# p doubled earlier, the first W_in tiles in pairs by column half, idle products placed anew, and a new order of the words, in an attention and MLP kernel

## The chip, the cores and the metric

The kernel runs on one core of one Trainium2 chip. TensorE does the products, VectorE, ScalarE and GpSimd (POOL) the rest, and SyncE (SP) starts the output and transposing DMAs. The metric is device time in microseconds (us). The kernel before takes 259.2 us, the median of 7 runs (258.06 to 260.01).

## What is computed

```
def sm_attn(qq, kk, vv):               # softmax attention, scale 1/sqrt(64)
    ...
p_packed = sm_attn(p, k, v)            # 32 packed rows of each head
out = sm_attn(q, p_packed, p_packed)   # (8, 8, 576, 64)
x = out.transpose(0, 2, 1, 3).reshape(4608, 512)
h = x @ w_in                           # 512 x 2048
r = np.maximum(h, 0.0)
g = s * (r * r) + b
y = g @ w_out                          # 2048 x 512
```

8 batches, 8 heads, 576 rows, 64 columns in a head. All is given and returned in float32; the kernel computes in bf16 with float32 sums.

## The kernel before

Batches are done one after another, interleaved on TensorE by an order written out by hand: a list of words (lines 583 to 610), each run by `run` (line 509), which issues that step's instructions on every engine. Within an engine the order of the words is the order of execution; nothing is rearranged. The words, with the functions they call:

- `Lk`, `Lq`, `Lv`, `Lwi`, `Lwo`, `Lpall`, `Lsb`: loads, all started by POOL (lines 109 to 141). `Lwi` and `Lwo` load a quarter of W_in or W_out. k, q and v of batch 0, and p of batch 0, are started ahead of the list.
- `Tk`, `Tq`: transposes of half of k or q on TensorE (`on_pe`, line 185) through a PSUM tile, copied by VectorE to kT or qT. `Dk`, `Dq` do it by a transposing DMA from SP (`on_dma`, line 205), from batch 2 on.
- `PP`: p of batch 0 is doubled by VectorE (`twice`, line 146), transposed on TensorE and copied by ScalarE to pbd (line 149). `PPA` does the same for the p of batches 1 to 7 (pall, line 164); there VectorE and ScalarE each make two copies of the PSUM tile.
- `V`: v reordered to vr by VectorE (line 212).
- `F`: first scores for 4 heads, and their exp to e1 on ScalarE (line 220).
- `P`: packed products and their sums (line 244); behind the second half VectorE and ScalarE make rd, ppd and rs.
- `S`: second scores, and their exp to e2 (line 279). For batch 0 they are laid out by column half (of the 576 rows of q), so that the first half can go on alone.
- `A`: sums over each head's 32, then Ln and Exp on ScalarE and a product on VectorE, giving aT (lines 315 and 332).
- `W`: W_in times the packed values, scaled to pw (`packed_w`, line 344). For batch 0 one quarter at a time through two single-bank PSUM tiles (tag "y"), for the others two quarters through two double-bank tiles (tag "h").
- `M`: one tile of 128 of the 2048 columns: four products of pw and aT into a PSUM tile, Relu to rlu, square to gT (line 398). ScalarE does Relu, except for batch 0 where m % 4 = 2: there VectorE does.
- `h` (batch 0 alone): the same tile by column half, `h0.m.half` (line 381). Words `h0.0.0 h0.1.0`, then `h0.0.1 h0.1.1`; each is two products, a Relu and a square of 288 columns. M0.2 and M0.3 follow whole.
- `B`: products of W_out with ones for the bias; behind the last VectorE scales it by b to biasrep (line 422).
- `Ob.tx n`: n of the 16 products of one output tile; behind the sixteenth VectorE scales, adds biasrep and SP stores (line 445).
- `Z n`: n idle products of 128x512 zeros into a PSUM tile of their own (`idle`, line 498).

Two PSUM pools set what may run ahead. Tag "h" has two double-bank tiles (`big`, line 77): every T, PP, PPA, F, S, A, M and h takes one, so a step waits until the step two tiles earlier has been read out. Tag "y" has four single-bank tiles for O, B, P, Z and batch 0's W. gT and W_out are kept whole in SBUF; pw, aT and two kT and qT are double.

Of the kernel before, what the change touches and what calls it, by code (L numbers as in the profile page):

```python
# [14 lines left out]
def kernel(  # L15
# [18 lines left out]
    P = 128  # L34
# [26 lines left out]
    def mm(*a, **kw):  # L61
        return tc.keep_in_program_order(nc.tensor.matmul(*a, **kw))  # L62
# [11 lines left out]

    vec, act, pool, sp = (Pinned(e) for e in (nc.vector, nc.scalar, nc.gpsimd, nc.sync))

    def big(dt=F32):
        return psh.tile([P, 2, NB if dt == F32 else 2 * NB], dt, tag="h", name="hps")


# [65 lines left out]
    def twice(t):  # L146
        vec.tensor_copy(out=t[:, :, 1, :], in_=t[:, :, 0, :])

    def prep_p0():
        twice(pn)  # L150
        pt = big(BF16)
        for x in range(2):
            tr(
                pt[:, 0, x * P:(x + 1) * P],
                pn[:, x, :, :],
                identb[:],
            )
        for c2 in range(2):
            act.copy(
                out=pbd[D * c2:D * c2 + D, :, 0, :, c2, :],  # L160
                in_=pt[D * c2:D * c2 + D, 0, 0:2 * P].rearrange("p (g a j) -> p a g j", g=4, a=2),
            )
# [113 lines left out]
        rs[b] = smp.tile([P, 2], F32, tag="rs", name="rs")  # L276
        vec.tensor_scalar_mul(out=rs[b][:], in0=rd[b][:], scalar1=scale)

    def second_scores(b, by_half=False):
        e2[b] = attp.tile([P, 2, S], BF16, tag="e2", name="e2")  # L280
        tiles = [big() for _ in range(2)]
        for a in range(2):
            for g in range(4):
                for c2 in range(2):
                    t, i = (c2, a) if by_half else (a, c2)
                    mm(
                        tiles[t][NP * g:NP * g + NP, i, 0:HS],
                        ppd[b % 2][D * c2:D * c2 + D, a, g, :],
                        qT[b % 2][D * c2:D * c2 + D, head(a, g), :, :],
                        start=True,  # L290
                        stop=True,
                        tile_position=(D * c2, NP * g),
                    )
        if by_half:
            exp_half(b, tiles, 0, 0)
            exp_half(b, tiles, 1, 0)
            s2[b] = tiles
            return
        for a in range(2):
            act.activation(  # L300
                out=e2[b][:, a, :].rearrange("p (i s) -> p i s", i=2),
                in_=tiles[a][:, :, 0:HS],
                func=AF.Exp,
                scale=rs[b][:, a:a + 1],
            )
# [38 lines left out]
    def packed_w(b, chs):  # L344
        if chs[0] == 0:
            pw[b] = atp.tile([P, 2, DFF], BF16, tag="pw", name="pw")
        if len(chs) == 2:
            at = {(a, x): (a, x) for a in range(2) for x in range(2)}
            tiles = [big() for _ in range(2)]
        else:  # L350
            at = {(a, 0): (a, 0) for a in range(2)}
            tiles = [psy.tile([P, 1, NB], F32, tag="y", name="wps") for _ in range(2)]
        for x, ch in enumerate(chs):
            for g in range(4):
                for a in range(2):
                    t, i = at[a, x]
                    mm(
                        tiles[t][NP * g:NP * g + NP, i, :],
                        ppd[b % 2][D * a:D * a + D, a, g, :],
                        w_in_sb[D * a:D * a + D, g, ch * NB:(ch + 1) * NB],  # L360
                        start=True,
                        stop=True,
                        tile_position=(D * a, NP * g),
                    )
        for a in range(2):
            t, i0 = at[a, 0]
            src = tiles[t][:, i0:i0 + len(chs), :]
            dst = pw[b][:, a, chs[0] * NB:(chs[-1] + 1) * NB].rearrange("p (i f) -> p i f", f=NB)
            if a == 0 and (b, chs[0]) != (0, 0):
                act.activation(out=dst, in_=src, func=AF.Copy, scale=rd[b][:, a:a + 1])  # L370
            else:
                vec.tensor_scalar_mul(out=dst, in0=src, scalar1=rd[b][:, a:a + 1])


    def slot(b):
# [3 lines left out]
        return 0 if (b % 4) in (1, 2) else NT * P  # L379

    def mlp_in_half(b, m, hf):
        if hf == 0:
            pps[b, m] = big()
        hps = pps[b, m]
        for a in range(2):
            mm(
                hps[:, hf, 0:HS],
                pw[b][:, a, m * P:(m + 1) * P],
                aT[b][:, a, hf * HS:(hf + 1) * HS],
                start=(a == 0),  # L390
                stop=(a == 1),
            )
        rlu = ysp.tile([P, HS], BF16, tag="rluh", name="rluh")
        act.activation(out=rlu[:], in_=hps[:, hf, 0:HS], func=AF.Relu)
        g0 = slot(b) * S + hf * HS
        vec.tensor_tensor(out=gT[:, m, g0:g0 + HS], in0=rlu[:], in1=rlu[:], op=ALU.mult)

    def mlp_in(b, m):
        hps = big()
# [98 lines left out]
    def idle(n, cols=P):  # L498
# [3 lines left out]
        for _ in range(n):  # L502
            mm(zps["t"][:, 0:cols], zb[:, 0:P], zb[:, 0:cols], start=True, stop=True)


    todo = {(b, t): o for b in range(B) for t, o in enumerate(outs(b))}
    todo[B - 1, NT].cuts = (0, NB // 2, NB)

    def run(word):
        what = word.rstrip("0123456789.x-")  # L510
        n = [int(x) for x in word[len(what):].replace("x", ".").replace("-", ".").split(".") if x]
        if what == "Z":
            idle(n[0], NB)
        elif what in ("Lk", "Lq", "Lv"):
            h0, h1 = (4 * n[1], 4 * n[1] + 4) if len(n) == 2 else (0, H)
            load(what[1], n[0], h0, h1)
# [7 lines left out]
            load_w_out(4 * n[0], 4 * n[0] + 4)  # L524
        elif what == "Lsb":
            load_sb()
        elif what == "PP":
            prep_p0()
        elif what == "PPA":
# [51 lines left out]
    idle(12, NB)  # L581

    for word in """
        Lwi0 Lwi1 Lwi2 Lwi3 Lwo0 Lwo1 Lpall Tk0.0 Z10 Tk0.1 Lk1 Lwo2 PP0 V0.0 Z7 F0.0 F0.1 V0.1 Z5 P0.0
        P0.1 Tq0.0 Tq0.1 Lq1 Lwo3 Lv1 Lsb Z4 S0 Z1 W0.0 A0.0 W0.1 A0.1 h0.0.0 h0.1.0 W0.2 h0.0.1 h0.1.1
        M0.2 M0.3 W0.3 M0.4 M0.5 M0.6 B0-4 M0.7 M0.8 O0.0x2 M0.9 B4-8 M0.10 M0.11 O0.0x3 PPA Tk1.0
        O0.0x3 O0.1x5 B8-12 Tk1.1 Lk2 M0.12 O0.0x3 F1.0 F1.1 O0.0x1 O0.1x2 Tq1.1 O0.1x1 Tq1.0 B12-16
        M0.13 O0.0x1 O0.1x5 V1 Lv2 Lq2 M0.14 M0.15 O0.0x1 P1.0 P1.1 O0.0x1 O0.1x1 O0.0x1 O0.1x2 S1
        O0.2x4 A1.0 O0.2x3 W1.0 O0.2x3 V2 O0.2x3 A1.1 O0.2x3 O0.3x1 W1.2 O0.3x5 Dq2 Dk2 Lk3 Lv3 Lq3
        O0.3x1 M1.0 O0.3x5 M1.1 M1.2 O0.3x2 M1.3 M1.4 O0.3x2 M1.5 M1.6 O1.0x2 M1.7 M1.8 O1.0x2 M1.9  # L590
        M1.10 O1.0x2 M1.11 M1.12 O1.0x2 M1.13 M1.14 O1.0x1 M1.15 F2.0 O1.0x2 F2.1 O1.0x5 P2.0 O1.1x1
        P2.1 O1.1x5 W2.0 O1.1x6 S2 O1.1x4 A2.0 O1.2x3 W2.2 O1.2x4 V3 O1.2x2 A2.1 O1.2x7 O1.3x4 M2.0 M2.1
        O1.3x2 Dq3 Dk3 Lk4 Lv4 Lq4 M2.2 M2.3 O1.3x2 M2.4 M2.5 O1.3x2 M2.6 M2.7 O1.3x2 M2.8 O1.3x4 M2.9
        M2.10 O1.4x2 M2.11 M2.12 O1.4x2 M2.13 M2.14 O1.4x2 M2.15 O1.4x7 F3.0 F3.1 O1.4x3 O2.0x3 P3.0
        P3.1 O2.0x5 W3.0 O2.0x6 W3.2 O2.0x2 O2.1x4 S3 O2.1x4 A3.0 O2.1x4 V4 O2.1x4 A3.1 O2.2x13 M3.0
        M3.1 Dq4 Dk4 Lk5 Lv5 Lq5 O2.2x2 M3.2 M3.3 O2.2x1 O2.3x1 M3.4 M3.5 O2.3x2 M3.6 M3.7 O2.3x2 M3.8
        M3.9 O2.3x2 M3.10 M3.11 O2.3x2 M3.12 M3.13 O2.3x2 M3.14 M3.15 O2.3x5 O3.0x3 F4.0 F4.1 O3.0x6
        P4.0 P4.1 O3.0x4 W4.0 O3.0x3 O3.1x3 W4.2 O3.1x6 S4 O3.1x5 A4.0 O3.1x2 A4.1 O3.2x1 V5 O3.2x14
        M4.0 M4.1 O3.2x1 O3.3x1 M4.2 Dq5 Dk5 Lk6 Lv6 Lq6 M4.3 O3.3x2 M4.4 M4.5 O3.3x2 M4.6 O3.3x11 M4.7
        M4.8 O3.4x2 M4.9 M4.10 O3.4x2 M4.11 M4.12 O3.4x2 M4.13 M4.14 O3.4x5 F5.0 F5.1 O3.4x5 M4.15 P5.0  # L600
        P5.1 O4.0x5 W5.0 O4.0x6 W5.2 O4.0x5 O4.1x1 S5 O4.1x3 A5.0 O4.1x3 V6 A5.1 O4.1x9 O4.2x6 M5.0 M5.1
        O4.2x1 Dq6 Dk6 Lk7 Lv7 Lq7 O4.2x1 M5.2 M5.3 O4.2x2 M5.4 M5.5 O4.2x2 M5.6 M5.7 O4.2x2 M5.8 M5.9
        O4.2x2 M5.10 M5.11 O4.3x2 M5.12 M5.13 O4.3x14 M5.14 M5.15 O5.0x2 F6.0 O5.0x1 F6.1 O5.0x5 P6.0
        O5.0x1 P6.1 O5.0x5 W6.0 O5.0x2 O5.1x4 W6.2 O5.1x6 S6 O5.1x5 V7 A6.0 O5.1x1 O5.2x1 A6.1 O5.2x14
        M6.0 M6.1 Dq7 Dk7 O5.2x1 M6.2 M6.3 O5.3x2 M6.4 M6.5 O5.3x2 M6.6 M6.7 O5.3x2 M6.8 M6.9 O5.3x2
        M6.10 M6.11 O5.3x2 M6.12 M6.13 O5.3x2 M6.14 M6.15 O5.3x4 O5.4x3 F7.0 F7.1 O5.4x6 P7.0 O5.4x1
        P7.1 O5.4x5 W7.0 O5.4x1 O6.0x5 W7.2 O6.0x6 S7 O6.0x4 A7.0 O6.0x1 O6.1x2 A7.1 O6.1x13 M7.0 M7.1
        O6.1x1 O6.2x1 M7.2 M7.3 O6.2x2 M7.4 M7.5 O6.2x2 M7.6 M7.7 O6.2x2 M7.8 M7.9 O6.2x2 M7.10 M7.11
        O6.2x2 M7.12 M7.13 O6.2x5 M7.14 M7.15 O6.3x16 O7.0x16 O7.1x16 O7.2x16 O7.3x16 O7.4x16
    """.split():  # L610
        run(word)
    while not todo[B - 1, NT].done:
# [29 lines left out]
```

## Time and profile before

| | |
|---|---|
| seven runs | 258.06, 258.63, 258.92, 259.2, 259.26, 259.83, 260.01 us |
| profiled execution: its time, its span | 258.06 us, 256.3 us |
| busy: TensorE, weight loads | 245.7 us (96%), 139.0 us (54%) |
| busy: VectorE, ScalarE, POOL | 143.4, 144.3, 29.7 us |
| granted TensorE clock, mean | 0.993 |
| output products, one M | 592 in 143.8 us; 512 in 76.0 us, four to an M |
| DMA | 35.47 MB, mean 138 GB/s |
| TensorE waits, longest | 1.2 us on zeros at the start, 1.0 us on pn, 0.9 us on pall, 0.8 us on W_in, 0.7 us on e (two) |

A line of the profile names the engine, the operation, out<-in with the program's tile names, the count and the time. All engine instructions but TensorE's have line 73, that of a helper, so they are told apart by tile: hps are the "h" tiles, yps outputs and bias, pps the packed products, wps batch 0's W, zps the idle products. Products are pipelined, and their ends are modelled: two lines next to each other can overlap by about 0.16 us, and a small gap shows as later starts and not as idle time. Times are from the start of the span.

### The profile page before, as it was taken

What the parts mean: (1) busy time and instruction counts of PE and PEld (TensorE: products, weight loads), DVE (VectorE), ACT (ScalarE), POOL (GpSimd) and SP (SyncE); (2) the same over time, 40 slices, a digit from 0 to 9 for tenths busy, and PEclk for the clock granted to TensorE, in tenths of its full rate; (3) what the DMA queues carried; (4) which work ended last, traced back from release to release, by engine and by line L of the source; (5) the groups of instructions that cost most, each with busy time, mean ns of one, the idle gap of its engine ahead of it and who ended that gap; (6) DMA issues with size and microseconds to landing.
All of it is one profiled execution on the core that took longest, in us unless ns stands there. A gap on an engine that the chain in (4) does not pass through costs nothing.

```text
span 256.3 us, 5247 instructions
## 1 busy us (share of the span) xinstructions
PE 245.7 (96%) x2169; PEld 139.0 (54%) x2169; DVE 143.4 (56%) x273; ACT 144.3 (56%) x231; POOL 29.7 (12%) x44
## 2 busy tenths in 40 slices
PE   8886989999999999999999999999999999999994
PEld 3452556546654665456635664465546654665453
DVE  4437874777656663566456556656366635664221
ACT  2158516386857774658466575684576847681000
POOL 8742301200200021002100030002000000000000
PEclk9997999999999999999999999999999999999999
DMA  6999999797798669957991679867997811111332
GB/s 84 171 206 207 194 205 203 95 216 164 141 177 184 133 133 168 193 115 153 169 193 43 137 135 201 154 134 140 195 162 130 138 43 42 48 37 41 82 84 82
DMA packets 59208, 35.47 MB, mean 138 GB/s; under 512 B 31920, under 2 KB 54704, under 8 KB 59184
## 3 DMA queue, kind: packets, MB, share of 16 engines
q0 software_dynamic: 25232, 18.62, 49.4%
q1 hardware_dynamic: 33952, 16.52, 28.9%
q8 instruction: 17, 0.28, 0.4%
q14 instruction: 7, 0.06, 0.1%
HBM read 37.23 MB, written 9.44 MB: 182 GB/s over the span
## 4 chain that ended last, share of the span: by engine, by line
PE 79%; DMA 16%; DVE 2%; POOL 1%; issue 1%; ACT 0%; POOLq 0%; DVEq 0%; ACTq 0%
PE yps L62 47%; PE hps L62 30%; DMA w_out_sb<-in_moe_w_out_dram 7%; DMA bvec<-in_moe_b_dram 6%; DMA vn<-in_v_dram 3%; PE pps L62 2%; POOL kn L73 1%; DVE gT L73 0%; DVE vr L73 0%; POOL pn L73 0%; DVE rlu L73 0%; POOL vn L73 0%; DVE biasrep L73 0%; ACT ppd L73 0%; DVE ppd L73 0%
## 5 line engine op out<-in xcount | busy, mean ns | idle before, releaser
L62 PE MATMUL yps<-w_out_sb,gT 128*128 128x512 bf16 (+1 forms) x592 | 143.8, 374 | 0.0
L73 ACT ACTIVATE rlu<-hps 128x576 bf16<-128x576 f32 x122 | 73.4, 648 | 38.3 <-PE hps L62 38.3
L62 PEld LDWEIGHTS <-gT 128*128 128x128 bf16 x592 | 55.0, 98 | 50.5 <-issue 6.7
L62 PE MATMUL hps<-aT,pw 128*128 128x288 bf16 x512 | 76.0, 288 | 1.6 <-DVE aT L73 0.4
L73 DVE TENSOR_TENSOR gT<-rlu 128x576 bf16<-128x576 bf16 x126 | 57.1, 458 | 32.9 <-ACT rlu L73 28.7
L62 PEld LDWEIGHTS <-pw 128*128 128x128 bf16 x512 | 50.0, 98 | 29.6 <-issue 3.6
L73 DVE SCALAR_TENSOR_TENSOR ysb<-yps,svec,biasrep 128x512 f32<-128x512 f32 (+1 forms) x37 | 27.0, 732 | 24.4 <-PE yps L62 16.3
L73 DVE TENSOR_TENSOR aT<-e,rcd 128x576 bf16<-128x576 bf16 x16 | 12.1, 755 | 17.9 <-ACT rcd L73 17.9
L73 POOL DMA_DIRECT2D kn<-in_k_dram x9 | 6.9, 769 | 128.9 <-DMA kT<-kn 94.9
L73 DVE TENSOR_SCALAR pw<-hps,rd 128x1024 bf16<-128x1024 f32 x14 | 18.0, 1282 | 5.3 <-PE hps L62 4.9
L73 ACT ACTIVATE pw<-hps,rd 128x1024 bf16<-128x1024 f32 x14 | 15.6, 1114 | 7.4 <-PE hps L62 7.3
L73 ACT ACTIVATE e<-hps 96x768 bf16<-96x768 f32 x16 | 12.0, 802 | 6.0 <-PE hps L62 6.0
L73 ACT ACTIVATE e<-hps,rs 128x576 bf16<-128x576 f32 (+1 forms) x18 | 11.4, 683 | 4.4 <-PE hps L62 4.3
L73 ACT CAST ppd<-pps 64x128 bf16<-64x128 f32 x16 | 4.2, 260 | 15.9 <-DVE ppd L73 15.9
L62 PE MATMUL zps<-zb 128*128 128x512 bf16 x39 | 11.5, 443 | 1.2 <-DVE zb L73 1.2
L62 PEld LDWEIGHTS <-ppd 64*32 64x32 bf16 x384 | 5.4, 89 | 12.6 <-issue 11.2
L73 ACT ACTIVATE ld<-hps 128x576 f32<-128x576 f32 x16 | 10.3, 646 | 2.2 <-PE hps L62 1.9
L73 ACT ACTIVATE rcd<-ld 128x576 f32<-128x576 f32 x16 | 10.9, 683 | 0.5
L62 PE MATMUL hps<-w_in_sb,ppd 64*32 64x512 bf16 x224 | 10.3, 381 | 0.0
L73 ACT COPY pbd<-hps 64x256 bf16<-64x256 bf16 (+1 forms) x4 | 2.4, 634 | 12.5 <-PE hps L65 8.5
L62 PEld LDWEIGHTS <-vr 96*128 96x128 bf16 x192 | 7.3, 97 | 3.1 <-issue 1.4
L62 PE MATMUL pps<-e,vr 96*128 96x64 bf16 x192 | 8.1, 192 | 0.3 <-ACT e L73 0.2
(56 smaller groups left out, 123.3 us busy)
## 6 DMA issues: line engine op xcount, KB each, us to landing
out_dram<-ysb SPq DMA_DIRECT2D x23, 192.0 KB, 2.3
kn<-in_k_dram POOLq DMA_DIRECT2D x7, 576.0 KB, 6.4
qn<-in_q_dram POOLq DMA_DIRECT2D x7, 576.0 KB, 11.8
vn<-in_v_dram POOLq DMA_DIRECT2D x7, 576.0 KB, 9.8
out_dram<-ysb SPq DMA_DIRECT2D x24, 128.0 KB, 2.5
w_in_sb<-in_moe_w_in_dram POOLq DMA_DIRECT2D x4, 512.0 KB, 13.7
w_out_sb<-in_moe_w_out_dram POOLq DMA_DIRECT2D x4, 512.0 KB, 19.0
out_dram<-ysb SPq DMA_DIRECT2D x23, 64.0 KB, 2.0
```

Source lines behind the costliest of these rows:

```text
L62: return tc.keep_in_program_order(nc.tensor.matmul(*a, **kw))
L73: return lambda *a, **kw: tc.keep_in_program_order(f(*a, **kw))
```

## The change

- `twice(pn)` is no longer part of `PP` but a word of its own, `PD`, and stands ahead of `Tk0.1`; VectorE doubles p before the second kT copy.
- `mlp_in_half` takes two neighbouring tiles m, m + 1 of one column half: four products into one "h" tile, one Relu and one square of 576 columns. The words are now `h0.2.0`, `h0.0.0`, `h0.2.1`, `h0.0.1`, so M0.2 and M0.3 are no longer whole tiles. VectorE does Relu for `h0.0.0`.
- A new word `Y n` does idle products into the "h" tile that the next step will use: `idle_in_next` takes the tile, and `big` hands it on.
- `packed_w` can do any number of quarters, and `second_scores` has a flag for W_in's first quarter; the words don't use either in a new way.
- The list of words is new from end to end. There are 42 Z and 7 Y products where there were 39 Z. `Lwo2` stands ahead of `Lpall` and `Lk1`. In batches 1 and 3 both W, and in 2, 5, 6 and 7 the second W, stand behind the second A (before, all W stood ahead of it but W1.2), and the two A are closer to each other.

The diff, with the list cut behind batch 1:

```
     def big(dt=F32):
+        if early:
+            return early.pop()
         return psh.tile([P, 2, NB if dt == F32 else 2 * NB], dt, tag="h", name="hps")
...
     def prep_p0():
-        twice(pn)
         pt = big(BF16)
...
     def mlp_in_half(b, m, hf):
-        if hf == 0:
-            pps[b, m] = big()
-        hps = pps[b, m]
-        for a in range(2):
-            mm(
-                hps[:, hf, 0:HS],
-                pw[b][:, a, m * P:(m + 1) * P],
-                aT[b][:, a, hf * HS:(hf + 1) * HS],
-                start=(a == 0),
-                stop=(a == 1),
-            )
-        rlu = ysp.tile([P, HS], BF16, tag="rluh", name="rluh")
-        act.activation(out=rlu[:], in_=hps[:, hf, 0:HS], func=AF.Relu)
+        hps = big()
+        cols = slice(hf * HS, (hf + 1) * HS)
+        for i in range(2):
+            for a in range(2):
+                mm(
+                    hps[:, i, 0:HS],
+                    pw[b][:, a, (m + i) * P:(m + i + 1) * P],
+                    aT[b][:, a, cols],
+                    start=(a == 0),
+                    stop=(a == 1),
+                )
+        rlu = ysp.tile([P, 2, HS], BF16, tag="rlu", name="rlu")
+        if hf == 0 and m == 0:
+            vec.tensor_scalar_max(out=rlu[:], in0=hps[:, :, 0:HS], scalar1=0.0)
+        else:
+            act.activation(out=rlu[:], in_=hps[:, :, 0:HS], func=AF.Relu)
         g0 = slot(b) * S + hf * HS
-        vec.tensor_tensor(out=gT[:, m, g0:g0 + HS], in0=rlu[:], in1=rlu[:], op=ALU.mult)
+        vec.tensor_tensor(out=gT[:, m:m + 2, g0:g0 + HS], in0=rlu[:], in1=rlu[:], op=ALU.mult)
...
+    def idle_in_next(n):
+
+        if not early:
+            early.append(big())
+        for _ in range(n):
+            mm(early[0][:, 0, :], zb[:, 0:P], zb[:, 0:NB], start=True, stop=True)
...
-        Lwi0 Lwi1 Lwi2 Lwi3 Lwo0 Lwo1 Lpall Tk0.0 Z10 Tk0.1 Lk1 Lwo2 PP0 V0.0 Z7 F0.0 F0.1 V0.1 Z5 P0.0
-        P0.1 Tq0.0 Tq0.1 Lq1 Lwo3 Lv1 Lsb Z4 S0 Z1 W0.0 A0.0 W0.1 A0.1 h0.0.0 h0.1.0 W0.2 h0.0.1 h0.1.1
-        M0.2 M0.3 W0.3 M0.4 M0.5 M0.6 B0-4 M0.7 M0.8 O0.0x2 M0.9 B4-8 M0.10 M0.11 O0.0x3 PPA Tk1.0
-        O0.0x3 O0.1x5 B8-12 Tk1.1 Lk2 M0.12 O0.0x3 F1.0 F1.1 O0.0x1 O0.1x2 Tq1.1 O0.1x1 Tq1.0 B12-16
-        M0.13 O0.0x1 O0.1x5 V1 Lv2 Lq2 M0.14 M0.15 O0.0x1 P1.0 P1.1 O0.0x1 O0.1x1 O0.0x1 O0.1x2 S1
-        O0.2x4 A1.0 O0.2x3 W1.0 O0.2x3 V2 O0.2x3 A1.1 O0.2x3 O0.3x1 W1.2 O0.3x5 Dq2 Dk2 Lk3 Lv3 Lq3
-        O0.3x1 M1.0 O0.3x5 M1.1 M1.2 O0.3x2 M1.3 M1.4 O0.3x2 M1.5 M1.6 O1.0x2 M1.7 M1.8 O1.0x2 M1.9
-        M1.10 O1.0x2 M1.11 M1.12 O1.0x2 M1.13 M1.14 O1.0x1 M1.15 F2.0 O1.0x2 F2.1 O1.0x5 P2.0 O1.1x1
...
+        Lwi0 Lwi1 Lwi2 Lwi3 Lwo0 Lwo1 Lwo2 Lpall Tk0.0 Z10 PD Tk0.1 Lk1 PP0 Z3 F0.0 V0.0 F0.1 Z5 P0.0
+        V0.1 P0.1 Tq0.0 Z3 Tq0.1 Lq1 Lwo3 Lv1 Lsb Z3 S0 Z2 W0.0 Z1 A0.0 Z3 W0.1 Y1 A0.1 Y1 h0.2.0 Y3
+        h0.0.0 W0.2 h0.2.1 Y2 h0.0.1 M0.4 W0.3 M0.5 M0.6 M0.7 B0-4 M0.8 M0.9 O0.0x2 M0.10 B4-8 M0.11
+        M0.12 O0.0x2 B8-12 M0.13 M0.14 O0.0x2 M0.15 O0.0x3 PPA Tk1.1 O0.0x3 O0.1x6 Tq1.0 O0.1x1 Tq1.1
+        O0.1x1 Tk1.0 Lk2 B12-16 O0.0x1 F1.0 F1.1 O0.0x1 V1 Lv2 Lq2 O0.0x2 O0.1x3 P1.0 O0.1x1 P1.1 O0.1x4
+        O0.2x1 S1 O0.2x5 A1.0 O0.2x2 A1.1 O0.2x6 W1.0 V2 O0.2x2 O0.3x8 W1.2 O0.3x3 Dq2 Dk2 Lk3 Lv3 Lq3
+        O0.3x3 M1.0 O0.3x1 M1.1 O0.3x1 M1.2 O1.0x1 M1.3 M1.4 O1.0x1 M1.5 M1.6 O1.0x1 M1.7 O1.0x1 M1.8
+        M1.9 O1.0x1 M1.10 O1.0x1 M1.11 O1.0x1 M1.12 O1.0x1 M1.13 O1.0x1 M1.14 O1.0x1 M1.15 O1.0x1 F2.0
+        O1.0x1 F2.1 O1.0x4 O1.1x1 P2.0 O1.1x1 P2.1 O1.1x5 W2.0 O1.1x6 S2 O1.1x3 O1.2x2 A2.0 O1.2x2 A2.1
+        O1.2x6 W2.2 V3 O1.2x6 M2.0 O1.3x2 M2.1 M2.2 O1.3x2 M2.3 O1.3x2 Dq3 Dk3 Lk4 Lv4 Lq4 O1.3x10 M2.4
...
```

## The prediction

> **What bounds the kernel now.** I read the page's slices first, then the chain of work that ended last, then TensorE's waits and its timeline.
>
> ```profile
> PE   8886989999999999999999999999999999999994
> PEclk9997999999999999999999999999999999999999
> ```
>
> TensorE is full from slice 8 on (51 us) and the only clock loss is in slice 3. So after batch 1 has begun the time is the sum of TensorE's products, 576 output products of 0.216 us among them, and the change can only win in the first 50 us, or by removing small gaps behind them. The chain says what those 50 us wait for:
>
> ```profile
> 30.70 15.32 DMA bvec<-in_moe_b_dram
> 46.11 0.54 DVE biasrep L73
> 46.78 0.45 DVE gT L73
> 47.23 0.87 DVE vr L73
> ```
>
> Columns: start, length, what. The loads form one queue that moves about 205 GB/s from 12 to 46 us (187 from 28 to 32); v of batch 1 lands at 45.70 and b at 46.02. VectorE then makes biasrep, one gT and vr (ends 48.10), and batch 1's packed products (P1.0) start at 48.15. **Everything ahead of P1.0 is worth nothing beyond that floor.**
>
> I counted the words ahead of P1.0 in both orders: all 16 M0, the bias products, PPA, both Tk1, Tq1 and F1, and 27 output products, in both. So the end moves by the shift of P1.0 plus the change of the gaps behind it.
>
> **Ahead of P1.0, part by part.** All work lies on the same three in-order engines, so I carry the starts through with this trace's durations.
>
> *p doubled early (PD).* On VectorE the 0.18 us copy moves ahead of the second kT copy. p lands at 8.26, the transposes for that kT copy end at 9.2: hidden (if p came 1 us later, kT and F0.0 would slip by that). It removes the wait of 0.95 us before the pn transposes. F0.0 goes from 11.80 to 10.2 (pbd copies: 10.49 less 0.3 after the transposes, 0.74 long), S0's last part from 17.61 to 16.1. But then comes W0.0, whose W_in quarter lands at 17.16 (18.30 before), and W0.1, whose quarter lands at 20.21: TensorE waits until 20.25 as it does now. Most of the 1.5 us is lost to DMA.
>
> *Behind W0.1.* ScalarE and VectorE set the pace: Ln 21.3 (21.71 before, as e is done earlier), rcd 21.95, aT 22.67 to 23.43, gT, Relu of h0.0.0 on VectorE to 24.5, then Y2, h0.0.1 25.0, M0.4 25.5, M0.5 26.45, M0.6 26.95, M0.7 28.1 (its PSUM buffer waits for M0.5's Relu, which stands behind the W0.3 copy on ScalarE), the bias products, M0.8 29.4 (30.30 before). The four tiles in pairs cost what the eight halves and two whole ones cost: ScalarE 3 x 0.65 = 1.95 against 4 x 0.41 + 0.65 = 2.3 us, VectorE 0.75 + 4 x 0.46 against 0.75 + 4 x 0.31 + 2 x 0.46. From M0.8 to M0.15's end TensorE is dense: 8 M of 0.49, 8 bias and 6 output products of 0.216, so 29.4 + 6.95 = 36.4.
>
> *pall, W_out and k.* Lwo2 passes Lpall and Lk1 in POOL's queue; the bytes up to v of batch 1 are the same, so v and b land as now. From the gaps between the landings (2.55 us a quarter, pall 1.46, k 2.93) W_out's third quarter comes at 33.0 (37.33), 0.7 before the bias products that need it, pall at 34.4 (31.87), k at 37.4 (34.80). Pall has 3 us of cover, as the next row shows. Lk2 goes behind the later Tk1.0, from 40.17 to 45.1; k2's transposing DMA starts at 63.08 on SP now, and q2 and v2 go out behind V1 as before, so nothing waits for it. The same holds for the later batches, whose loads move by a few products and are needed over 10 us on.
>
> ```profile
> 35.30 0.91 PE L65 MATMUL hps<-identb,pall 112*128 112x112 bf16 x15 [0.93 <-DVE pall L73]
> 40.22 0.65 PE L62 MATMUL hps<-aT,pw 128*128 128x288 bf16 x4 [0.35 <-ACT pbd L73]
> ```
>
> The first row: pall's doubling stands on VectorE behind the gT of the last M before it, and M0.11's end (33.56) to pall's start on TensorE took 1.74 us. Now that M is M0.15: 36.4 + 1.74 = 38.1, while only three output products cover it. The second row: PPA's PSUM buffer came free 4.92 us after 35.30. The next user of that buffer is now Tq1.0: 38.1 + 4.92 = 43.0, with Tk1.1 and nine output products (2.5 us) under it, about 1.5 us idle. Then Tq1.0, Tq1.1 (43.75), Tk1.0 (44.55), the kT copy (ends 46.0), F1.0 46.1, and e of F1.1 2.1 us after F1.0 starts (11.80 to 13.90 in batch 0): **P1.0 at 48.2**. biasrep waits for the last bias products (46.2), vr ends 47.9: no longer last. Against 48.15: **+0.1**.
>
> *Idle products.* 39 Z become 42 Z and 7 Y: ten more, at 0.216 us 2.2 us, each in a wait. Y is not in this trace: it writes the PSUM tile that the next product needs, so Y3 waits for the Ln of A0.1 (22.0), and h0.0.0 and W0.2 queue behind its 0.65 us. Bound: nothing, to 0.65 us on the chain above; I take nothing, as Relu of h0.0.0 waits for VectorE until 23.7 anyway. What they are to keep is the clock:
>
> ```profile
> 15.66:19.07 3.41, 2.69 (x41) 1.20 (x38) 1.98 (x5) 1.99 (x6) 1.10 (x2) 1.00 1.23 205
> 19.07:22.48 3.41, 1.77 (x15) 0.74 (x15) 2.53 (x4) 3.25 (x7) 0.79 (x1) 1.00 1.24 207
> 22.48:25.90 3.42, 3.04 (x18) 1.27 (x18) 2.48 (x6) 2.66 (x6) 0.81 (x2) 0.50 1.25 207
> ```
>
> Columns: stretch, length, busy TensorE, weight loads, VectorE, ScalarE, POOL, granted clock, DMA. A stretch busy for 1.77 of 3.41 us (52%) is followed by 3.42 us at half clock; the least busy one that is not is 8.83 to 12.24 with 2.46 (72%). With W, Y, A, Y, h and Y from 20.25 on I get about 2.2 us (65%), nearer to 72: full clock. If halved, M0.2 to M0.4 give the price: 12 products in 2.68 us instead of 1.47, so 1.2; at most half of 3.42, 1.7.
>
> The Trainium skill ("TensorE: Matmul & The Clock Gate", section "Why this matters for your kernels") asks only for no idle gap over about 3 us; the longest gap here was 1.0 us and the clock halved all the same. By that rule the idle products would be worth nothing; the row decides. The same page (Part 1) calls the window free-running, which would let the halved stretch fall elsewhere in other executions.
>
> **Behind P1.0.** The gaps in TensorE's starts beyond the product's own length, from the timeline. Each O-to-W and O-to-S turn costs 0.09, unchanged in number. What the two PSUM buffers allow is seen here:
>
> ```profile
> 67.79 0.59 PE L62 MATMUL yps<-w_out_sb,gT 128*128 128x512 bf16 x2
> 68.22 1.14 PE L62 MATMUL hps<-aT,pw 128*128 128x288 bf16 x8
> 69.20 0.38 PE L62 MATMUL yps<-w_out_sb,gT 128*128 128x512 bf16 x1
> 69.62 0.65 PE L62 MATMUL hps<-aT,pw 128*128 128x288 bf16 x4
> ```
>
> M1.13 starts at 68.22, M1.15 (same buffer) at 69.62: 1.40 later, the fill of 0.65 plus Relu of 0.65 plus two hand-overs. Two M fill 0.98, so two output products just fit; here there is one, and 0.20 is lost though no idle is shown.
>
> - Batch 1's M: the new order has 12 output products in 15 spaces, three short: 3 x 0.2, and F2.1 0.13. Before 0.2 + 0.12. **+0.4**
> - S1: before 0.15 + 0.27 lost (an output product for gT, S for ppd); now ppd's second ScalarE cast ends about 0.1 after TensorE comes to it. **-0.3**. S3 now stands five products behind P3 too: **+0.1**
> - W six products behind the second A (six batches): Ln ends 1.67 us after A starts (190.69 to 192.36), TensorE comes after 1.63: 0.05 each, **+0.3**; W4's 0.08 goes.
> - P six products behind F: 0.11 each, five times instead of four: **+0.1**. A5.0 (0.15), M6.2 (0.20) and some 0.08 of M pairs go: **-0.5** with W4.
>
> Sum: +0.1 +0.4 -0.3 +0.1 +0.3 +0.1 -0.5 = **+0.2 us**. The profiled execution took 258.06 us (span 256.3, 1.8 around it): 258.3. It is the lowest of seven; the median is 259.2, so I put 259.2 + 0.2 = **259.4 us**.
>
> **Rivals.**
> - *The clock, for us (faster).* 258.06 to 260.01 is a wide spread, and before, TensorE reached P1.0 with 0.3 us to spare (last output product issued at 47.63, 0.216 long). If the halved stretch costs more in most executions than in the profiled one (up to 1.7 instead of 1.2 us, or a second stretch), the median holds a loss that the profile hardly has, and the change removes it: back to 258.06 + 0.2 = 258.3, -0.9. For: the longer busy run from 20.25. Against: the DMA floor hides losses of the first 46 us, and DMA may make the spread.
> - *The clock, against us (slower).* In the new order P1.0 hangs on the work behind W0.1 and on PPA, not on DMA. If the products don't hold the clock, 1.2 us go between 22 and 26, where every Relu and W copy waits for TensorE, less about 0.2 that the buffers hide: 260.4. It decides where that stretch is under some 60% busy, or when 1.5 us idle behind PPA halves the clock at 43.
> - *The gaps (slower).* My chain from 20.25 to 48.2 has some forty hand-overs; 0.05 us each missed is 1 us, as is PPA one buffer later: 260.3.
> - *It does next to nothing.* What PD and the pairs win is waited away for W_in and for v: P1.0 at its floor of 47.9, the gaps behind it as many as now: -0.25, 258.95 on the median. Within 0.3%.
>
> **Numbers.** Measurement can tell 0.3%, 0.8 us. Forecast (with the fourth case) 0.45, within 258.5 to 260.0. Clock for us 0.26. Clock against us 0.15, gaps 0.14: slower 0.29. The range reaches to both sides, 258.0 to 260.7; the far end of the 1.7 us bound (261.1) is in what is left out.
>
> **What would show it.** Right: clock 1.00 from 19 to 30 us; TensorE idle about 1 us before PPA and 1.5 us before Tq1.0; v landing at 45.7; P1.0 at 48.2; three starts 0.2 us late among M1. Wrong: a clock of 0.5 anywhere after 6 us; P1.0 below 47.5 (then v or b landed earlier) or above 49; a gap over 0.3 us behind 55 us.

## The result and the profile after

| | before | changed |
|---|---|---|
| median (range, runs) | 259.2 us (257.99 to 261.78, 47) | 258.09 us (257.62 to 258.56, 19) |
| ratio | | 0.9954, 95% interval 0.9942 to 0.9967 |
| profiled execution: time, span | 258.06, 256.3 us | 258.13, 256.0 us |
| P1.0 starts; from there to the last output product's start | 48.15; 204.30 us | 48.16; 204.02 us |

The change makes the kernel faster by 0.46%, 1.1 us. The prediction, 259.4 us, was wrong: it expected no difference, and put 0.26 on a gain of this size. The two profiled executions differ by 0.07 us, so most of what the medians gained can't be found by laying these two profiles side by side. Two opposite things stand behind the 0.07: the span is 0.3 us shorter, and the time outside the span (device time less span) is 0.35 us longer. The second holds in all executions, about 1.7 to 1.8 us before and 2.1 to 2.2 changed; what takes it is not shown.

The page of the changed kernel, TensorE's busy time and granted clock in 40 slices:

```profile
PE   8898989999999999999999999999999999999994
PEclk9999999999999999999999999999999999999999
```

Slice 3 has full clock now. The chain of work that ended last, around P1.0 (start, length, what):

```profile
31.04 15.35 DMA bvec<-in_moe_b_dram
46.39 0.03 issue
...
46.48 0.76 DVE biasrep L73
47.24 0.04 DVEq L73
47.28 0.83 DVE vr L73
48.11 0.05 issue
48.16 0.65 PE pps L62 x18
```

P1.0 is at the same place, behind the same end: b lands, VectorE makes biasrep and vr. But one piece is missing: before, the gT of M0.13 stood between biasrep and vr. From b's landing to P1.0 it takes 1.77 us now (46.39 to 48.16), where it took 2.13 (46.02 to 48.15). Here b landed 0.37 us later, so the two starts agree by chance. What else differs stands in TensorE's timeline, with the idle time ahead of a line in brackets:

```profile
38.20 0.96 PE L65 MATMUL hps<-identb,pall 112*128 112x112 bf16 x16 [1.04 <-DVE pall L73]
...
42.00 0.67 PE L65 MATMUL hps<-identb,qn 96*128 96x96 bf16 x12 [0.38 <-DVE kT L73]
42.51 0.38 PE L62 MATMUL yps<-w_out_sb,gT 128*128 128x512 bf16 x1
43.13 0.67 PE L65 MATMUL hps<-identb,qn 96*128 96x96 bf16 x12 [0.24 <-ACT pbd L73]
...
46.15 1.46 PE L62 MATMUL yps<-w_out_sb,gT 128*128 128x512 bf16 x6
48.16 0.52 PE L62 MATMUL pps<-e,vr 96*128 96x64 bf16 x12 [0.55 <-DVE vr L73]
```

The last row is the one to keep in mind: TensorE has done all else and is idle for 0.55 us ahead of P1.0. Behind P1.0, one output product between two M costs what was expected:

```profile
62.68 0.38 PE L62 MATMUL yps<-w_out_sb,gT 128*128 128x512 bf16 x1
62.90 1.33 PE L62 MATMUL hps<-aT,pw 128*128 128x288 bf16 x8
64.06 0.38 PE L62 MATMUL yps<-w_out_sb,gT 128*128 128x512 bf16 x1
```

The eight products of two M take 1.16 us, from 62.90 to the next start at 64.06; where two output products stand between, two M fill 0.98.

### The profile page after: what moved, and what is told of

Read it like the earlier page. It is cut to its first block, busy times and chain, and to the rows that moved or that the text cites. A ratio compares the mean times of both kernels' runs of the same rounds, so it can differ in the third digit from the quotient of the medians.

```text
span 256.0 us, 5264 instructions
## 1 busy us (share of the span) xinstructions
PE 245.9 (96%) x2179; PEld 138.7 (54%) x2179; DVE 143.4 (56%) x271; ACT 144.9 (57%) x229; POOL 29.7 (12%) x44
## 3 DMA queue, kind: packets, MB, share of 16 engines
q0 software_dynamic: 25232, 18.62, 49.3%
## 4 chain that ended last, share of the span: by engine, by line
PE 80%; DMA 16%; POOL 1%; DVE 1%; issue 1%; POOLq 0%; DVEq 0%
PE yps L62 47%; PE hps L62 30%; DMA w_out_sb<-in_moe_w_out_dram 7%; DMA bvec<-in_moe_b_dram 6%; DMA vn<-in_v_dram 3%; PE pps L62 3%; POOL kn L73 1%; DVE vr L73 0%; DVE biasrep L73 0%; POOL pn L73 0%; POOL vn L73 0%; DVE ysb L73 0%; POOL identb L73 0%; POOLq L73 0%; DVEq L73 0%
## 5 line engine op out<-in xcount | busy, mean ns | idle before, releaser
L62 PE MATMUL yps<-w_out_sb,gT 128*128 128x512 bf16 (+1 forms) x592 | 145.6, 374 | 0.0
L73 ACT ACTIVATE rlu<-hps 128x576 bf16<-128x576 f32 x124 | 75.7, 649 | 26.6 <-PE hps L62 25.8
L73 DVE TENSOR_TENSOR gT<-rlu 128x576 bf16<-128x576 bf16 x128 | 57.7, 457 | 27.8 <-ACT rlu L73 24.4
L62 PE MATMUL zps<-zb 128*128 128x512 bf16 x42 | 12.6, 436 | 1.2 <-DVE zb L73 1.2
L73 DVE RECIPROCAL rd<-pps 128x2 f32<-128x2 f32 x8 | 1.4, 171 | 14.9 <-PE pps L62 14.9
```

Of the source, the lines that this page charges most:

```text
L73: return lambda *a, **kw: tc.keep_in_program_order(f(*a, **kw))
```

## The experiments

Theory after the result: before, most executions run as the profiled one did not, with more half clock between 20 and 30 us, which TensorE's chain passes on to P1.0; the changed prefix (all ahead of P1.0) swallows it. Rivals: the idle products keep the clock; the part behind P1.0 brings the gain; one part alone (p, pairs, order) does. Ratios are to the kernel before, timed beside it in the same set of runs, with 95% intervals. There were five such sets after the first result, and the median of before went from 258.87 to 259.43 us between them, so kernels of different sets are compared by their ratios. Where no line of the list is shown, the rest is as in the kernel named.

### How typical the profiled execution was, and the clock

**before_again**: no edit.

> The kernel before, unchanged, to see many executions with the clock of each. The two profiled executions differ by 0.3 us of span, the medians by 1.1 us, so the median of before must hold a loss that its profiled execution hardly has. Clock theory: the mean granted clock is below 1 in every execution, it differs between executions (one half-clock stretch is 1 - 0.5 x 3.41/256 = 0.993, two are 0.987), and the slower executions are those with the lower clock; median 259.2. DMA theory: the clock is the same in all, and the time follows the landing of v or b of batch 1 (45.7 to 46.0 in the profile).

258.99 us, 0.9997 (0.9979 to 1.0015). The profiled execution, 258.65 us, had two stretches of half clock, not one. TensorE's, then the other engines' busy time, and the clock, by stretch:

```profile
18.38:21.80 3.42, 1.76 (x22) 0.73 (x22) 2.26 (x4) 3.29 (x8) 0.82 (x2) 1.00 1.25 205
21.80:25.21 3.41, 2.99 (x17) 1.07 (x17) 2.51 (x6) 3.05 (x8) 0.76 (x1) 0.50 1.24 206
25.21:28.63 3.42, 3.42 (x20) 1.62 (x20) 2.44 (x6) 1.64 (x3) 1.06 (x2) 0.50 1.25 206
```

P1.0 starts at 48.93, and the chain to it holds no DMA from 26 us on:

```profile
36.38 0.97 PE hps L65 x16
37.35 0.02 issue
37.37 2.09 DVE pbd L73 x2
...
39.54 1.72 ACT pbd L73 x2
41.26 0.04 issue
41.30 0.65 PE hps L62 x4
...
46.60 1.29 PE yps L62 x6
47.89 0.98 PE hps L62 x8
48.87 0.05 issue
48.93 1.14 PE pps L62 x36
```

PPA stands 1.08 us later than in the profile shown first, M0.12 waits for its copies as there, and TensorE is dense to P1.0; vr had ended at 48.65. From P1.0 to the last output product's start it takes 204.10 us. Over the executions of the kernel before in this set whose mean clock is 0.987, which is two such stretches, the median is 259.10 us (27 of them); at 0.993, one stretch, 258.42 (9); the one at 1.00 took 258.04. So the second stretch goes with 0.7 us here; in the three other sets with both kinds it is 0.25, 0.7 and 0.55 us (with 6, 2 and 2 executions at 0.993). The profile that the prediction was made from had the rarer, faster kind. The one shown here is faster than the median of its own kind, too, so in a median execution P1.0 should start later than 48.93, about 49.3 by the difference in time (an estimate; no profile shows it).

**before_fill**: ten idle products between A0.0 and W0.2 of the kernel before.

```
-S0 Z1 W0.0 A0.0 W0.1 A0.1 h0.0.0 h0.1.0 W0.2
+S0 Z1 W0.0 A0.0 Z4 W0.1 Z2 A0.1 Z1 h0.0.0 Z1 h0.1.0 Z2 W0.2
```

> The kernel before with ten more idle products between A0.0 and W0.2 and no other change: no p doubled early, no pairs, the old order. Clock theory: clock 1.00 in nearly all executions, 258.0 to 258.4, that is 0.9957 of before, and the spread falls below 1 us. DMA theory and the theory that the new order wins: no change or slower, 259.2 to 259.6, as the ten products only stand in waits.

258.79 us, 1.0004 (0.9981 to 1.0026). The clock was kept in 8 executions of 12 (0.998 or more), with a median of 258.57. The other four, at 0.993, took 260.08 to 260.43. The profiled one is of these: its half stretch came at 51 us, where nothing covers it (205.6 us from P1.0 to the last output product's start). Ahead of it TensorE was idle for 1.50 us: b landed at 47.09 and P1.0 started at 49.22, 2.13 later as in the first profile, behind biasrep, that gT and vr. Keeping the clock alone doesn't give the gain.

**after_bare**: the changed kernel without 11 of its idle products.

```
-W0.0 Z1 A0.0 Z3 W0.1 Y1 A0.1 Y1 h0.2.0 Y3 h0.0.0 W0.2 h0.2.1 Y2 h0.0.1
+W0.0 A0.0 W0.1 A0.1 h0.2.0 h0.0.0 W0.2 h0.2.1 h0.0.1
```

> The changed kernel without the seven Y and without the four Z around A0.0: p early, the pairs and the new order stay. Clock theory: a half-clock stretch is back behind 22 us, clock 0.993 or less, 258.8 to 259.5 and the wide spread again. Rival (pairs, early p and order are the gain): 258.1 as with the idle products, whatever the clock does, because P1.0 waits for v anyway.

258.06 us, 0.9957 (0.9936 to 0.9978). Half clock is back, as the page shows:

```profile
PEclk9997999999999999999999999999999999999999
```

and the time isn't: 258.07 in the six executions at 0.993, 257.95 in the five at 1.00. The one at 0.985 took 258.07. In the changed order a halved stretch at this place costs 0.12 us, and in the profiled execution TensorE still waits 0.42 us for vr ahead of P1.0. **The rival of the idle products falls**, for one halved stretch; two are seen in no_pairs below.

### Which side of P1.0

**old_new**: the kernel before up to P1.0, the changed order behind. **new_old**: the changed kernel up to P1.0, the old order behind. **after_b1**: the changed kernel with the old order from P1.0 to P2.0 alone (and one more output product ahead of M1.15). The seam of new_old:

```
-P1.0 O0.1x1 P1.1 O0.1x4 O0.2x1 S1 O0.2x5 A1.0 O0.2x2 A1.1 O0.2x6 W1.0 V2
+P1.0 P1.1 O0.1x5 S1 O0.2x4 A1.0 O0.2x3 W1.0 O0.2x3 V2 O0.2x3 A1.1 O0.2x3
...
```

> The kernel before up to P1.0, the changed order from P1.0 on. Theory now: before, a typical execution has two half-clock stretches between 21 and 29 us, which push P1.0 from 48.15 to 48.9, and the changed order ahead of P1.0 has slack that swallows them; behind P1.0 both orders cost the same to 0.3 us. Then this stays within 0.3 us of before, 258.6 to 259.0, its time still follows the clock (0.987 slower than 0.993 by 0.7), and from P1.0 to the last product it takes 204.0. Rival (the gain lies behind P1.0): 258.1.

> The changed kernel up to P1.0, the old order from P1.0 on. If everything of the gain lies ahead of P1.0: 258.1 or a little above, 0.996 of before, from P1.0 to the last product 204.1 to 204.3, no dependence on the clock. If the new order behind P1.0 is needed: 258.9.

> The changed kernel with the old order from P1.0 to P2.0 of batch 1 (one output product moved ahead of M1.15). By the rule of the two PSUM buffers the three starts 0.2 us late and F2.1's go, and S1 keeps its 0.25: 0.4 to 0.6 us less than the changed kernel, 257.6, 0.994 of before. If an output product more or less between two M doesn't set the pace: 258.1.

old_new 259.49 us, 1.0015 (1.0000 to 1.0029). new_old 257.41 us, 0.9945 (0.9930 to 0.9961). after_b1 257.60 us, 0.9945 (0.9925 to 0.9965). The gain lies ahead of P1.0. From P1.0 to the last output product's start the profiled executions take 204.02 us in the changed kernel, 204.13 in new_old, 203.64 in after_b1: behind P1.0 the new order is worth 0.1, made up of a loss of 0.4 in batch 1 and a gain of 0.5 behind it. new_old has the lower median all the same: 0.36 us of that lies outside the span, 1.78 us as in the kernel before instead of 2.14. The intervals of the two ratios overlap.

old_new is not a clean test. At its seam an output product of the changed order, between P1.0 and P1.1, waits 0.29 us for a gT that the old order makes behind vr, and from P1.0 on it takes 204.45 us instead of the 204.0 expected.

### One part alone

**pd_only**: the kernel before with p doubled early and the new words up to A0.0. **order_only**: the kernel before with `Lwo2` early and the new order from M0.4 on. **no_pairs**: the changed kernel with the old halves, M0.2 and M0.3 whole, and without Y and the Z1 and Z3 around A0.0. **old_ppa**: p early and pairs, without those idle products, then the old order from W0.3 to P1.0 and the loads as before. What order_only changes ahead of P1.0:

```
-M0.6 B0-4 M0.7 M0.8 O0.0x2 M0.9 B4-8 M0.10 M0.11 O0.0x3 PPA Tk1.0 O0.0x3 O0.1x5 B8-12 Tk1.1 Lk2 M0.12
-O0.0x3 F1.0 F1.1 O0.0x1 O0.1x2 Tq1.1 O0.1x1 Tq1.0 B12-16 M0.13 O0.0x1 O0.1x5 V1 Lv2 Lq2 M0.14 M0.15
+M0.6 M0.7 B0-4 M0.8 M0.9 O0.0x2 M0.10 B4-8 M0.11 M0.12 O0.0x2 B8-12 M0.13 M0.14 O0.0x2 M0.15 O0.0x3
+PPA Tk1.1 O0.0x3 O0.1x6 Tq1.0 O0.1x1 Tq1.1 O0.1x1 Tk1.0 Lk2 B12-16 O0.0x1 F1.0 F1.1 O0.0x1 V1 Lv2 Lq2
```

> The kernel before with p doubled early and the changed words up to A0.0, nothing else. If DMA holds W0.1 at 20.2 to 20.4 as computed, F0.0 to S0 come 0.5 to 1.5 us earlier and nothing behind W0.1 does: 258.7 to 259.1, two half-clock stretches as before. Rival (early p is the gain): P1.0 at 48.1 in spite of the clock, 258.1.

> The kernel before up to M0.4 (p doubled late, eight halves, M0.2 and M0.3 whole, no Y), W_out's third quarter ahead of pall and the changed order from M0.4 on. If the order alone gives the slack: as the kernel without pairs, 258.3, 0.998 of before, and P1.0 at 48.2 to 48.6. If early p was part of it: 259.0 or more, P1.0 at 49.

> The changed order and early p, but the eight halves and whole M0.2 and M0.3 of before in place of the pairs, and no Y. If the place of PPA (behind all of M0, W_out's third quarter ahead of pall) gives the slack: P1.0 at the end of vr, 258.0 to 258.3, and no dependence on the clock. If the pairs give it: 258.8 to 259.3, P1.0 at 48.7 or later, PPA at 38.8 or later.

> Early p and the pairs (no Y), then the old order from M0.4 to P1.0, with PPA behind M0.11 and the loads as before; from P1.0 the changed order. If the pairs give the slack: P1.0 at the end of vr, 258.0 to 258.3. If the place of PPA does: 258.7 to 259.1 and the time follows the clock.

| kernel | p early | pairs | order to P1.0 | us | ratio (95%) | P1.0, profiled |
|---|---|---|---|---|---|---|
| pd_only | yes | no | old | 258.91 | 1.0004 (0.9978 to 1.0030) | 48.40 |
| order_only | no | no | new | 259.64 | 1.0032 (1.0006 to 1.0059) | 49.50 |
| old_ppa | yes | yes | old | 259.25 | 1.0024 (1.0001 to 1.0048) | 48.99 |
| no_pairs | yes | no | new | 258.28 | 0.9982 (0.9967 to 0.9997) | 48.53 |
| after_bare | yes | yes | new | 258.06 | 0.9957 (0.9936 to 0.9978) | 48.20 |

No part alone wins, and the profiles show why. With early p alone (pd_only) TensorE waits 0.69 us ahead of P1.0, and P1.0 starts 2.14 us behind the landing of b (46.26) as before: the gT of M0.13 still stands between biasrep and vr. With the new order alone (order_only) that queue is shorter, but PPA starts at 40.15, and TensorE comes last. With both (no_pairs) a part is gained. Its profiled execution has two halved stretches: vr ended at 48.16 and TensorE came to P1.0 at 48.53, so the slack was used up. after_bare has the pairs on top; that they give the rest is likely, but the two intervals overlap.

In old_ppa PPA starts at 34.45, the earliest of all, and P1.0 is late all the same. Its chain:

```profile
46.96 0.12 DVE biasrep L73
47.08 0.54 issue
47.61 0.45 DVE gT L73
48.06 0.87 DVE vr L73
48.93 0.68 DVE rlu L73
...
49.63 0.47 DVE gT L73
...
50.14 0.39 PE yps L62
```

vr stands on VectorE behind biasrep and the gT of M0.13, which the old order leaves to the last. That is the same queue as in the first profile, and an earlier PPA doesn't move it: b landed at 46.85, and P1.0 started at 48.99, 2.14 later, with TensorE idle for 2.04 us. The last rows are the seam again: the output product between P1.0 and P1.1 waits 0.51 us for a gT behind vr, and from P1.0 on it takes 204.67 us. So the seam is a part of what makes old_ppa slower than the kernel before. `Lwo2`'s place was not tried by itself.

### The slack, measured

Idle products between M0.7 and M0.8 delay all that TensorE does from 29 us on by a known amount. **before_z4**, **after_z4**, **after_z8**, **after_z2**; **after_again** is the changed kernel without an edit.

```
-B0-4 M0.7 M0.8 O0.0x2
+B0-4 M0.7 Z4 M0.8 O0.0x2
...
-M0.7 B0-4 M0.8 M0.9
+M0.7 B0-4 Z4 M0.8 M0.9
```

> The kernel before with four idle products (4 x 0.216 = 0.86 us of TensorE) between M0.7 and M0.8, ahead of PPA and P1.0. Theory (the old order has no slack ahead of P1.0, so it passes a delay of TensorE on in full): P1.0 near 49.5 to 49.8, median 259.6 to 260.0, +0.6 to +0.9. Rival (both orders have the same slack): the same shift as the changed kernel with four idle products in that place.

> The changed kernel with four idle products (0.86 us) between the first bias products and M0.8. Theory (0.55 us of TensorE's time are idle ahead of P1.0, waiting for vr): P1.0 48.2 to 48.6, median 258.1 to 258.4, +0.0 to +0.3. Rival (no slack): +0.9, 258.9.

> The changed kernel with eight idle products (1.73 us) in the same place. Theory: the slack of 0.55 us is used up and the rest shows, P1.0 near 49.3, +1.0 to +1.2, 259.1 to 259.3. Rival (no slack): +1.7, 259.8. If the slack were far larger than the idle time that the profile shows: no shift, 258.1.

> The changed kernel without an edit, beside the next one. Both theories: 258.0 to 258.2, ratio to before 0.995 to 0.998, clock 1.00 in nearly all executions.

> The changed kernel with two idle products (2 x 0.216 = 0.43 us of TensorE) between the first bias products and M0.8. Theory (0.55 us idle ahead of P1.0, waiting for vr): the delay fits under it, so the same time as the changed kernel beside it, within 0.1 us, P1.0 still released by vr. Rival (no slack in most executions): +0.4.

| kernel | delay | us | against its own kernel | ratio to before (95%) |
|---|---|---|---|---|
| before_z4 | 0.86 | 259.62 | +0.75 | 1.0029 (1.0016 to 1.0042) |
| after_z2 | 0.43 | 257.95 | +0.04 | 0.9929 (0.9902 to 0.9956) |
| after_again | | 257.91 | | 0.9932 (0.9906 to 0.9957) |
| after_z4 | 0.86 | 258.30 | +0.2 | 0.9978 (0.9968 to 0.9988) |
| after_z8 | 1.73 | 259.24 | +1.15 | 1.0012 (0.9992 to 1.0031) |

before_z4 and before (258.87) are of one set, and so are after_z2 and after_again; after_z4 and after_z8 are set against 258.09, which is of another set, where before stood at 259.2 instead of 258.87. By the ratios they would be +0.6 and +1.5. (The low ratios of after_z2 and after_again have to do with the kernel before, 259.43 there: 6 of its 23 executions had a mean clock of 0.98 and took 261 us or more.) Between themselves z4 and z8 differ by 0.94 for 0.86 of delay. So the old order passes a delay on nearly in full, and the new one swallows 0.43 whole and has nothing left at 0.86. How large its slack is, these rows tell only roughly: 0.2 to 0.7 us. TensorE's timeline in after_z4 shows it used up, P1.0 at 48.20 with no idle time ahead:

```profile
46.09 0.86 PE L62 MATMUL hps<-pbd,kT 128*128 128x64 bf16 x24
46.79 1.46 PE L62 MATMUL yps<-w_out_sb,gT 128*128 128x512 bf16 x6
48.20 0.51 PE L62 MATMUL pps<-e,vr 96*128 96x64 bf16 x12
```

### What is left

**after_v1**: in the changed kernel V1 goes ahead of the last bias products, so that vr doesn't stand behind biasrep's wait for b. **tuned**: that, after_b1, and one more output product between F and P of batches 3 to 7 and between P3 and S3. **tuned2**: tuned with V2 and the loads behind it moved.

```
-Tk1.0 Lk2 B12-16 O0.0x1 F1.0 F1.1 O0.0x1 V1 Lv2 Lq2
+Tk1.0 Lk2 V1 B12-16 O0.0x1 F1.0 F1.1 O0.0x1 Lv2 Lq2
...
-W1.0 O0.2x3 V2 O0.2x3 A1.1 O0.2x3 O0.3x1 W1.2 O0.3x5 Dq2 Dk2 Lk3 Lv3 Lq3 O0.3x1 M1.0 O0.3x5 M1.1 M1.2
+W1.0 O0.2x6 A1.1 O0.2x3 O0.3x1 W1.2 O0.3x5 Dq2 Dk2 O0.3x1 M1.0 O0.3x5 M1.1 M1.2 V2 Lk3 Lv3 Lq3
```

> The changed kernel with the word V1 moved ahead of B12-16, so that VectorE makes vr before biasrep. In the changed kernel P1.0 waits 0.55 us with TensorE idle: v lands at 46.05, b at 46.39, biasrep ends 47.2, vr 48.1. If that floor (and not TensorE) sets P1.0, vr ends at 47.1, e of F1.1 at 47.5, P1.0 starts at 47.5 to 47.6: 0.5 to 0.6 us less, 257.5, 0.994 of before. If TensorE's chain sets it: P1.0 at 48.1 and 258.1.

> The changed kernel with the old order in batch 1 (0.5 us), V1 ahead of B12-16 (0.5 us), and one more output product between F and P in batches 3 to 7 (5 x 0.11) and between P3 and S3 (0.23), each taken from where there are more than enough: 1.5 us less than the changed kernel if the gaps add up, 256.6, 0.990 of before. If the buffers or ScalarE take it back: 257.3.

> The kernel labelled tuned with batch 2's V (and the loads behind it) moved from ahead of A1.1 to behind M1.2, so that aT and pw of batch 1 don't queue behind vr's wait for v on VectorE. Theory (this wait of 2 us is what made tuned spread from 256.2 to 259.0): a narrow spread, median 256.2 to 256.6, 0.990. Rival (the spread comes from elsewhere): 257.6 as tuned.

after_v1 257.75 us, 0.9959 (0.9938 to 0.9979): in the profiled execution vr ended at 46.47 (47.1 expected) and P1.0 started at 47.39 (47.5 to 47.6), but the ratio shows no gain over the changed kernel; why is open. tuned 257.61 us, 0.9947 (0.9927 to 0.9966), missed the 256.6 expected and spread from 256.15 to 258.99. Its profiled execution, the slowest, shows what I had missed, on VectorE:

```profile
57.99 0.96 DVE L73 COPY vr<-vn 96x3072 bf16<-96x3072 bf16 x1 [2.92 <-DMA vn<-in_v_dram]
58.87 0.75 DVE L73 TENSOR_TENSOR aT<-e,rcd 128x576 bf16<-128x576 bf16 x1
```

vr for batch 2 waits 2.92 us for its load, aT of batch 1 stands behind it, and TensorE waits 1.92 us for aT before M1.1. In tuned2 aT comes at 56.13, and vr at 61.22 without a wait. tuned2 takes **256.27 us (255.86 to 256.8), 0.9897 (0.9876 to 0.9918)**, in the range expected; from P1.0 on it takes 202.80 us instead of the changed kernel's 204.02. It beats both kernels.

## Why the prediction was wrong

**The step that failed** is the last of the sum: "It is the lowest of seven; the median is 259.2, so I put 259.2 + 0.2". The shift was worked out from one execution and added to the median of others. But a median execution of the kernel before has a second half-clock stretch, worth 0.25 to 0.7 us, with P1.0 at 48.93 in before_again; and the changed order pays little for a delay there: 0.12 us for a halved stretch (after_bare), 0.04 for 0.43 us of idle products (after_z2). The profiled execution was favoured by its loads as well: b landed at 46.02, the earliest of the seven profiled executions with the old order of loads (to 47.09).

**Against its own execution the sum was near, by luck**: 258.3 worked out, 258.13 measured. The span was to grow by 0.2 us and shrank by 0.3; and "1.8 around it", taken over without a reason, became 2.1.

**The rival had the number and half of the cause.** "The clock, for us" gave 258.3. Its condition, a second stretch in most executions, is what before_again shows. But it put the gain down to "the longer busy run from 20.25", so to the products that keep the clock; after_bare has the halved stretch and keeps the gain. Two other things carry it: slack ahead of P1.0, 0.55 us in the changed kernel's profile, and the shorter queue on VectorE. The second is seen wherever vr releases P1.0: 2.13 to 2.14 us from b's landing in before, before_fill, pd_only and old_ppa, 1.76 to 1.77 in the changed kernel, after_again, after_z2, after_bare, after_b1 and new_old. The prediction had that shorter queue ("vr ends 47.9"), but as the last thing it took its own chain on TensorE, which hid it. No run changes that queue alone, so how much of the gain each of the two brings is not measured: in the set of after_bare the median span fell from 257.1 us to 255.9, and 0.4 more went outside it.

**"In the new order P1.0 hangs on the work behind W0.1 and on PPA, not on DMA"** was wrong, and with it the case against the change: vr came last, 0.55 us behind TensorE. Two steps of the chain made this: Tq1.0 was given PPA's buffer, free at 43.0, and started at 42.00 behind the kT copy; Tq1.1 was the one that had to wait, until 43.13. So the idle time behind PPA was 0.38 + 0.24 us instead of 1.5, F1.0 came at 45.45 instead of 46.1. And vr ended at 48.10 instead of 47.9, since b landed at 46.39, 0.37 later than before. That P1.0 stood at 48.16, where 48.2 was forecast, is luck: TensorE came 0.6 us earlier than forecast and vr 0.2 later.

**What held of the chain.** M0.8 29.4 (expected 29.4), PPA 38.20 (38.1) after 1.04 us idle (about 1). W_out's third quarter, pall and k landed at 33.30, 34.77 and 37.69 (33.0, 34.4, 37.4). The stretch from 18.89 to 22.30, which answers to the one that was busy for 52% before, was busy for 2.75 of 3.41 us at full clock.

**Behind P1.0**: +0.1 expected from there on, -0.28 measured between the two profiled executions. Three starts 0.195 late among M1, F2.1 0.12 and P 0.11 five times are as expected. The term that was mis-sized is W behind the second A, +0.3: no start of W was late beyond the turn of 0.093 that all have, and the steps between W's own products fell from 5.06 us in sum to 4.55. S1 and S3 lost 0.25 each instead of 0.1.

## What to carry to other kernels

Before a shift is added to a median, ask whether the profiled execution is a median one: here its time was the lowest of seven and its clock, 0.993, was that of 9 executions of 44. Where a transfer sets the end of a stage, work moved ahead of it isn't worth nothing: it is the slack that hides what varies, and a known delay put into both kernels shows which of them has it. Count what stands in the queue between the landing and the work that waits for it: one gT there was 0.36 us. Look on in-order engines for the copy whose load may be late, and for what stands behind it: moving one such copy (tuned2 against tuned) was worth about as much as the whole change, 0.5% by the ratios.

## What the runs showed of the hardware

- **How often the clock is halved differs between executions of one kernel**: of the 44 executions of the kernel before in the set of before_again, 27 had a mean of 0.987, 9 of 0.993, one of 1.00, and the other 7 lay from 0.98 to 0.992.
- **What a halved stretch goes with.** In the ten profiled executions that have one, the stretch of 3.41 us ahead of the first halved one was busy on TensorE for 1.61 to 2.08 us; up to 100 us none of 2.10 or more at full clock was followed by one. Of the halved stretches themselves, those busy for 2.17 to 3.00 us were followed by a second, those of 3.03 to 3.42 weren't. So 2.99 in before_again against 3.03 in the profile shown first is one stretch more.
- The page "TensorE: Matmul & The Clock Gate" of the Trainium skill (section "Why this matters for your kernels") asks for no idle gap over about 3 us. The runs here don't agree that this is enough: in the kernel before, the stretch ahead of the halved one had a longest gap of 0.8 us.
- **The floor of the loads moves too.** With the same loads ahead of it, P1.0 started at 48.16, 47.75 and 47.14 us in the profiled executions of the changed kernel, after_again and after_z2, each 0.05 to 0.06 behind the end of vr; b had landed at 46.39, 45.98 and 45.37.
